# Depthwise-separable 1x1 convolution: the weight-scaling prologue re-ordered, one transfer on another queue

## The chip, the cores and the metric

The kernel runs on one core of a Trainium2 chip. Its engines are TensorE (matrix multiplication, PE in the profile, with its weight loads as PEld), VectorE (DVE), ScalarE (ACT), GpSimd (POOL) and SyncE (SP, which here issues most transfers). The metric is the device time of one execution in microseconds; less is better. Before the change it is 573.41 us, the median of three runs (573.28 to 573.43).

## The reference

The input `x` is a bf16 image of 384 x 384 pixels with 384 channels, `dw` holds one factor per channel (a depthwise kernel of size 1), and `pw` is a 384 x 384 matrix:

```
out = x * dw[0, 0][None, None, None, :]      # depthwise, k = 1
out = einsum('bhwc,cd->bhwd', out, pw)       # pointwise
```

So the result is, for 147456 pixels, a row of 384 channels times a 384 x 384 matrix whose rows are scaled by `dw`.

## The kernel before, in words

The scaling is folded into the weights: the kernel first forms `w_r`, the rows of `pw` times `dw`, in an order that suits the main loop, and then multiplies `x` by it.

The main loop goes over 288 supertiles of 512 pixels. A supertile is loaded as a part of a chunk of `x` (chunks of 1, 1, 1, 1, 2, 4, 5, 5 and then 10 supertiles, at the end smaller ones again) into one of three buffers `X`. VectorE transposes it in 32 x 32 blocks of 32-bit words into one of two tiles `T` (`transposes`, L348 to L380); one instruction makes half a supertile, three of the six pairs of channel blocks. Only the first supertile's first half is made in three single blocks (L370 to L372), so that TensorE can begin after the first of them. TensorE then runs `supertile` (L220): 12 steps of 4 matmuls, each with 32 rows of the array and 384 columns, into four banks of one of the two PSUM tiles `PS`. ScalarE copies the four banks out as bf16 (L434), and SyncE issues the store. The order on each engine is the order in which the code issues to it; the semaphores hold the engines together. There is no planner.

Ahead of the loop stands a prologue of a few microseconds:

- ScalarE's queue loads `dw` (L183), SyncE's queue loads the first 128 rows of `pw` (L184), then the other 256 (L185, semaphore `s_pw2`), then the chunks of `x` (`load_x`, L133), one after the other.
- GpSimd makes an identity `eye`; VectorE sums it into the selector `sel` (L395, which raises `s_dwf` to 1).
- TensorE runs dummy matmuls over a constant (`idle_work`, L244; each pass is four matmuls): four passes, then, when `dw` has landed, three tiny matmuls that turn the row `dw` into columns of PSUM (L260), then three more passes.
- VectorE copies those columns from PSUM to `dw_f` (L402, `s_dwf` to 2) and makes three scaled selectors `sel_w`, one for each 128 rows of `pw` (L405, `s_sw`).
- TensorE multiplies `sel_w` and `pw` (L280), six products (k, r) for k in 0 to 2 and r in 0 and 1. The products (1, 1) and (2, 0) are run twice. Each leaves two banks of PSUM, and raises `s_w`.
- ScalarE and VectorE copy the products from PSUM into `w_r` (`w_out`, L387, with the copy on L390). The list of units and engines is `w_units` (L175): unit 0 on ScalarE, 1 on VectorE, 2 on ScalarE, the fourth product in two halves, one on ScalarE and one, `(3, 1, 2, 0)`, on VectorE, then 4 and 5 on ScalarE.
- VectorE then goes on with the first two supertiles' transposes. The loop's first matmul waits for the units of the first four products on both engines (`w_first`, `w_after(3)`) and for the first transposed block (`s_t[0][0]`).

The PSUM bank that held the columns of `dw` is also written by product (0, 0). Because each engine works in order, an instruction that waits on VectorE or on SyncE's queue holds all that is issued behind it there.

Of the kernel before, what the change touches and what calls it, by code (L numbers as in the profile page):

```python
# [26 lines left out]
def kernel(  # L27
# [12 lines left out]
    nc = tc.nc  # L40
    P = nc.NUM_PARTITIONS
    B, H, W, C = x.shape
    assert dw.shape[0] == 1 and dw.shape[1] == 1, "only k=1 depthwise supported"
    D = pw.shape[1]
# [29 lines left out]
    pw_n = raw[:, 0 : 3 * D].rearrange("p (k d) -> p k d", d=D)  # L74
    sel_w = raw[:, 3 * D :].rearrange("p (k r q w) -> p k r q w", r=2, q=4, w=32)
    w_k = raw[:, 0 : 2 * D].rearrange("p (r d) -> p r d", d=D)
    eye = consts.tile([P, P], BF16, name="eye")
    sel = consts.tile([P, 2, 32], F32, name="sel")
    w_r = consts.tile([P, NB, 2, D], BF16, name="w_r")
    dw_row = consts.tile([1, C], BF16, name="dw_row")  # L80
    dw_f = consts.tile([P, 3], F32, name="dw_f")
# [9 lines left out]
    PS = [psum.tile([P, 4, 512], F32, name=f"ps{s}") for s in range(2)]  # L91
# [13 lines left out]
    s_pw2 = nc.alloc_semaphore("s_pw2")  # L105
    s_df = nc.alloc_semaphore("s_df")
    s_sw = nc.alloc_semaphore("s_sw")
    s_dwf = nc.alloc_semaphore("s_dwf")
# [4 lines left out]
    with tc.tile_critical(sync_engine=mybir.EngineType.Pool, no_gpsimd_drain=True) as section:  # L113
        def x_of(t):
            g, i, off, first, L = chunks[t]
            if first + 2 == NS:
                return Xl[:], s_xl, 32
            n = sum(len(ls) > i for ls in groups[g % NR : g + 1 : NR])
            return Xs[g % NR][:, 4 * off : 4 * (off + L), :], s_x[g % NR][i], 16 * n

        def load_x(t, eng=nc.sync):
            g, i, off, first, L = chunks[t]
            dst, sem, _ = x_of(t)
            rows = xf[512 * first : 512 * (first + L), :]
            if first + 3 < NS:
                src = rows.rearrange("(p s) c -> p (s c)", p=P)
                dst = dst.rearrange("p s c -> p (s c)")
                if i == 0 and g >= NR:
                    je = g_end[g - NR]
                    eng.wait_ge(s_t[je % 2][1], je // 2 + 1)  # L130
            else:
                src = rows.rearrange("(a k q) c -> q a k c", k=4, q=4)
            eng.dma_start(dst, src).then_inc(sem, 16)  # L133
# [43 lines left out]
        def w_after(i):  # L177
            n = [sum(u[3] == e and u[0] <= i for u in w_units) for e in range(2)]
            return [(s_wr[e], n[e]) for e in range(2)]
# [2 lines left out]

        nc.scalar.dma_start(dw_row[:], dw.rearrange("a e c -> a (e c)")).then_inc(s_dw, 16)  # L183
        nc.sync.dma_start(pw_n[:, 0], pw[0:P, :]).then_inc(s_pw, 16)  # L184
        nc.sync.dma_start(pw_n[:, 1:3], pw[P:C, :].rearrange("(k p) d -> p k d", p=P)).then_inc(s_pw2, 16)  # L185
        load_x(0)

        todo = []
# [25 lines left out]
        def w_ps(i):  # L214
            return PS[0 if i in (2, 3) else 1][:, 2 * (i % 2) : 2 * (i % 2) + 2, :D]
# [28 lines left out]
        def idle_work(n):  # L244
            for _ in range(n):
                for i in range(4):
                    nc.tensor.matmul(  # L247
                        PS[0][:, 2 * (i % 2) + i // 2, :D],
                        lhsT=ones[32 * i : 32 * i + 32, 0:P],
                        rhs=ones[32 * i : 32 * i + 32, :],  # L250
                        start=True,
                        stop=True,
                        tile_position=(32 * i, 0),
                    )
# [3 lines left out]
        nc.tensor.wait_ge(s_dw, 16)  # L258
        for k in range(3):
            mm = nc.tensor.matmul(  # L260
                PS[1][:, 0, D + k : D + k + 1],
                lhsT=dw_row[:, P * k : P * k + P],
                rhs=ones[0:1, 0:1],
                start=True,
                stop=True,
            )
        mm.then_inc(s_df)
        idle_work(3)
        nc.tensor.wait_ge(s_pw, 16)
        times = {(1, 1): 2, (2, 0): 2}  # L270
        for k in range(3):
            if k == 1:
                nc.tensor.wait_ge(s_pw2, 16)
            nc.tensor.wait_ge(s_sw, k + 1)
            for r in range(2):
                if k == 2:
                    nc.tensor.wait_ge(*w_after(r)[1 - r])

                for v in [0, 1] * times.get((k, r), 1):
                    mm = nc.tensor.matmul(  # L280
                        PS[(k + 1) % 2][:, 2 * r + v, :D],
                        lhsT=sel_w[64 * v : 64 * v + 64, k, r, :, :].rearrange("p q w -> p (q w)"),
                        rhs=pw_n[64 * v : 64 * v + 64, k, :],
                        start=True,
                        stop=True,
                        tile_position=(64 * v, 0),
                    )
                mm.then_inc(s_w)
# [59 lines left out]
        def transposes(t, j):  # L348
            g, i, off, first, L = chunks[t]
            jj = first + j  # L350
            s = jj % 2
            if jj + 1 == NS:
                nc.vector.wait_ge(s_xk, 32)
                Tw = Ts[s][:].bitcast(U32).rearrange("p b (m w) -> p (b m) w", w=32)
                for v in range(2):
                    blocks = slice(12 * v, 12 * v + 12)
                    ins = nc.vector.transpose(out=Tw[:, blocks], in_=Xk[:, blocks].bitcast(U32))  # L357
                    ins._wait_ge(s_pe, 2 * (jj - 2) + v + 1)
                    ins.then_inc(s_t[s][v])
                return  # L360
            X, sem, n = x_of(t)
            Xw = X.bitcast(U32).rearrange("p (k l) c -> p k l c", l=L)
            Tw = Ts[s][:].bitcast(U32).rearrange(
                "p b (k i) -> p b k i" if t < 2 else "p b (i k) -> p b k i", k=4
            )
            for h in range(2):
                if h == 0 and j == 0:
                    nc.vector.wait_ge(sem, n)
                if h == 0 and jj == 0:
                    for b in range(3):  # L370
                        x_b = Xw[:, :, 0, 32 * b : 32 * b + 32]
                        nc.vector.transpose(out=Tw[:, b], in_=x_b).then_inc(s_tb if b else s_t[0][0])  # L372
                    continue
                ins = nc.vector.transpose(  # L374
                    out=Tw[:, 3 * h : 3 * h + 3],
                    in_=Xw[:, :, j, 96 * h : 96 * h + 96].rearrange("p k (b w) -> p b k w", w=32),
                )
                if jj >= 2:
                    ins._wait_ge(s_pe, 2 * (jj - 2) + h + 1)
                ins.then_inc(s_t[s][h])  # L380
# [6 lines left out]
        def w_out(i, v0, v1, e):  # L387
            k, r = i // 2, i % 2
            out, in_ = w_r[:, 2 * k + v0 : 2 * k + v1, r, :], w_ps(i)[:, v0:v1]
            o = nc.vector.tensor_copy(out, in_) if e == 0 else nc.scalar.copy(out, in_)  # L390
            o._wait_ge(s_w, i + 1)
            o.then_inc(s_wr[e])
# [5 lines left out]
            op=mybir.AluOpType.add,  # L398
            axis=mybir.AxisListType.X,
        ).then_inc(s_dwf)  # L400
        nc.vector.wait_ge(s_df, 1)
        nc.vector.tensor_copy(dw_f[:], PS[1][:, 0, D : D + 3]).then_inc(s_dwf)  # L402
        nc.vector.wait_ge(s_dwf, 2)
        for k in range(3):
            nc.vector.tensor_scalar_mul(  # L405
                sel_w[:, k], sel[:].unsqueeze(2).to_broadcast([P, 2, 4, 32]), dw_f[:, k : k + 1]
            ).then_inc(s_sw)
        for u in w_units:
            w_out(*u)
        transposes(*order[0])  # L410
        transposes(*order[1])

        for jj, (t, j) in enumerate(order):
# [29 lines left out]
            if jj + 2 < NS:  # L443
                transposes(*order[jj + 2])
# [35 lines left out]
```

## Time and profile before

| what | value |
|---|---|
| median of three runs | 573.41 us |
| the profiled execution | 573.63 us |
| its span, first to last instruction | 571.7 us |
| TensorE busy (matmuls) | 566.9 us |
| VectorE busy | 507.9 us |
| ScalarE busy | 418.4 us |
| bytes moved by the transfers | 226.88 MB, mean 397 GB/s |
| first matmul of the main loop | 6.45 us after the span's start |

The times are of one profiled execution, counted from its first instruction. In the rows of the order of time the first number is the start and the second the duration, then come engine, line, operation, output and inputs with their shapes, the number of instructions merged into the row, and in brackets the engine's idle time before it with what ended that. A `q` behind an engine's name marks an instruction of its queue that issues a transfer; it is not counted as busy time, and its duration is that of the issue, not of the transfer. Ends of matmuls are modelled, so a matmul's duration is longer than the distance to the next one. In the rows of groups, busy time and mean duration stand behind the bar.

### The profile page before, as it was taken

The page shows a single profiled execution, that of the slowest core. Times are in us where ns is not written, and L with a number is a line of the kernel's source. Part 1 is how long each engine was busy: PE and PEld are TensorE (multiplying, and loading weights), DVE is VectorE, ACT ScalarE, POOL GpSimd, SP SyncE. Part 2 cuts the span into 40 slices and gives each one's busy share as a digit, 9 for nine tenths or more (in the row PEclk, how much of TensorE's full clock was granted, in tenths as well). Part 3 has the DMA queues.
Part 4 walks back from the last instruction along what each step waited for, and adds up shares of the span by engine and source line. Part 5 has one row for each costly group of instructions (what it writes and reads, how often), then busy time and mean ns, then how long its engine had stood idle before and what let it go on. Part 6 is the DMA issues. An engine that isn't in the chain of part 4 may idle for free.

```text
span 571.7 us, 29724 instructions
## 1 busy us (share of the span) xinstructions
PE 566.9 (99%) x13847; PEld 414.4 (72%) x13847; DVE 507.9 (89%) x589; ACT 418.4 (73%) x298; POOL 13.9 (2%) x41
## 2 busy tenths in 40 slices
PE   8999999999999999999999999999999999999997
PEld 5777777777777777777777777777777777777775
DVE  7889889889889889899899898898898898898896
ACT  6777777777777777777777777777777777777775
POOL 2042000000000000000000000000000000000000
PEclk9999999999999999999999999999999999999999
DMA  8999999999999999999999999999999999998777
GB/s 320 440 385 390 434 422 429 433 421 418 421 439 414 399 405 425 403 393 393 434 387 390 408 413 404 407 411 412 406 404 415 402 395 397 423 393 330 307 286 270
DMA packets 28084, 226.88 MB, mean 397 GB/s; under 512 B 1449, under 2 KB 7850, under 8 KB 24106
## 3 DMA queue, kind: packets, MB, share of 16 engines
q1 hardware_dynamic: 27140, 225.91, 97.6%
q10 hardware_dynamic: 934, 0.89, 0.4%
q14 instruction: 9, 0.07, 0.0%
q8 instruction: 1, 0.02, 0.0%
HBM read 113.54 MB, written 113.25 MB: 397 GB/s over the span
## 4 chain that ended last, share of the span: by engine, by line
PE 99%; DVE 0%; ACT 0%; issue 0%
PE ps L230 98%; PE ps L247 0%; DVE w_r L390 0%; PE ps L315 0%; PE ps L280 0%; PE ps L303 0%; ACT O L429 0%; DVE T L372 0%; PE ps L260 0%
## 5 line engine op out<-in xcount | busy, mean ns | idle before, releaser
L230 PE MATMUL ps<-w_r,T 32*128 32x384 bf16 x13776 | 559.8, 321 | 0.3 <-DVE T L372 0.3
L374 DVE STREAM_TRANSPOSE T<-X 128x384 uint32<-128x384 uint32 x571 | 499.5, 876 | 55.2 <-DMA X<-in_x_dram 0.5
L230 PEld LDWEIGHTS ps<-w_r,T 32*128 32x128 bf16 x13776 | 411.3, 93 | 148.8 <-issue 0.9
L434 ACT CAST O<-ps 128x1536 bf16<-128x1536 f32 x286 | 411.7, 1440 | 146.6 <-PE ps L230 146.6
L344 POOL COPY Xk<-Xl 32x256 bf16<-32x256 bf16 x16 | 6.3, 396 | 0.0
L343 POOL COPY Xk<-Xl 32x128 bf16<-32x128 bf16 x16 | 4.6, 289 | 24.8 <-DMA Xl<-in_x_dram 24.0
L390 ACT CAST w_r<-ps 128x768 bf16<-128x768 f32 (+1 forms) x5 | 3.3, 754 | 1.2 <-PE ps L280 1.2
L247 PE MATMUL ps<-const-bfloat16-1.0 32*128 32x384 bf16 x28 | 2.7, 514 | 1.1 <-PEq L464 1.1
L338 POOL COPY raw<-w_r 32x768 bf16<-32x768 bf16 x4 | 3.3, 821 | 6.5 <-ACT w_r L390 6.3
L346 ACT ACT_TABLE_LOAD x1 | 1.3, 1283 | 1.5 <-PEq L464 1.5
L280 PE MATMUL ps<-raw 64*128 64x384 bf16 x16 | 2.4, 466 | 0.0
L425 DVE CAST O<-ps 128x384 bf16<-128x384 f32 x2 | 1.0, 554 | 1.4 <-PE ps L230 1.4
L280 PEld LDWEIGHTS ps<-raw 64*128 64x128 bf16 x16 | 1.0, 126 | 1.6 <-issue 1.3
L390 DVE CAST w_r<-ps 128x768 bf16<-128x768 f32 (+1 forms) x2 | 1.5, 758 | 0.7 <-PE ps L280 0.7
L247 PEld LDWEIGHTS ps<-const-bfloat16-1.0 32*128 32x128 bf16 x28 | 0.9, 121 | 1.6 <-issue 1.4
L374 DVE STREAM_TRANSPOSE T<-Xl 128x384 uint32<-128x384 uint32 x2 | 1.8, 882 | 0.2
L395 DVE TENSOR_REDUCE sel<-eye 128x64 f32<-128x128 bf16 x1 | 0.3, 289 | 1.5 <-POOL eye L325 1.5
L357 DVE STREAM_TRANSPOSE T<-Xk 128x384 uint32<-128x384 uint32 x2 | 1.2, 578 | 0.5 <-PE ps L230 0.4
L429 ACT CAST O<-ps 128x384 bf16<-128x384 f32 x2 | 1.0, 480 | 0.7 <-PE ps L315 0.7
L315 PE MATMUL ps<-raw,T 128*128 128x384 bf16 x8 | 1.5, 328 | 0.0
L429 DVE CAST O<-ps 128x384 bf16<-128x384 f32 x2 | 1.1, 558 | 0.1
L424 ACT CAST O<-ps 128x384 bf16<-128x384 f32 x2 | 0.9, 482 | 0.5 <-PE ps L230 0.5
(14 smaller groups left out, 5.1 us busy)
## 6 DMA issues: line engine op xcount, KB each, us to landing
X<-in_x_dram SPq DMA_DIRECT2D x25, 3840.0 KB, 21.8
out_dram<-O SPq DMA_DIRECT2D x25, 3840.0 KB, 27.7
X<-in_x_dram SPq DMA_DIRECT2D x3, 1536.0 KB, 18.5
X<-in_x_dram SPq DMA_DIRECT2D x2, 1920.0 KB, 14.5
out_dram<-O SPq DMA_DIRECT2D x2, 1920.0 KB, 24.0
out_dram<-O SPq DMA_DIRECT2D x2, 1536.0 KB, 13.0
X<-in_x_dram SPq DMA_DIRECT2D x6, 384.0 KB, 5.8
out_dram<-O SPq DMA_DIRECT2D x3, 768.0 KB, 5.7
```

Of the source, the lines that this page charges most:

```text
L230: mm = nc.tensor.matmul(PS[s][:, q, :D], lhsT=Ts[s][32 * q : 32 * q + 32, b, par::2], rhs=w_r[32 * q : 32 * q + 32, b, par, :], start=(b, ...
L247: nc.tensor.matmul(PS[0][:, 2 * (i % 2) + i // 2, :D], lhsT=ones[32 * i : 32 * i + 32, 0:P], rhs=ones[32 * i : 32 * i + 32, :], start=True ...
L280: mm = nc.tensor.matmul(PS[(k + 1) % 2][:, 2 * r + v, :D], lhsT=sel_w[64 * v : 64 * v + 64, k, r, :, :].rearrange("p q w -> p (q w)"), rhs ...
L315: mm = nc.tensor.matmul(PS[1][:, m, :D], lhsT=Tk[:, P * (m + 2) : P * (m + 3), par], rhs=w_k[:, par, :], start=False, stop=par == 1,)
L338: nc.gpsimd.tensor_copy(w_k[quads[n]], w_r[quads[n], n]).then_inc(s_wk)
L343: nc.gpsimd.tensor_copy(Xk[quads[n], g:8:4, :], x_b).then_inc(s_xk)
L344: nc.gpsimd.tensor_copy(Xk[quads[n], 8 + g : 24 : 4, :], Xl[quads[g], :, 64 * n : 64 * n + 64]).then_inc(s_xk)
L346: nc.scalar.copy(warm[:, s : s + 1], nc.const_aps.tensor(0.0, [P, 1], F32)).then_inc(s_a[s])
L374: ins = nc.vector.transpose(out=Tw[:, 3 * h : 3 * h + 3], in_=Xw[:, :, j, 96 * h : 96 * h + 96].rearrange("p k (b w) -> p b k w", w=32),)
L390: o = nc.vector.tensor_copy(out, in_) if e == 0 else nc.scalar.copy(out, in_)
L429: o = (nc.scalar.copy if n % 2 else nc.vector.tensor_copy)(Ov[:, n, j, :], PS[s][:, n, :D])
L434: a = nc.scalar.copy(Ov[:, :, j, :], PS[s][:, :, :D])
```

## The change

Six edits, all in the prologue:

1. The last 256 rows of `pw` are loaded from ScalarE's queue, behind `dw`, instead of SyncE's.
2. SyncE waits until VectorE's sum is done (`s_dwf` at 1) before it issues the first chunk of `x`; all later issues on that queue come behind it.
3. The columns of `dw` go to bank 2 of the second PSUM tile instead of bank 0, which product (0, 1) overwrites.
4. The second group of dummy passes has two instead of three.
5. VectorE scales the first selector with the column of `dw` taken from PSUM, then copies the columns to `dw_f`, then scales the other two from `dw_f`. Product (0, 1) waits until the copy is done (`s_dwf` at 2).
6. VectorE's half unit `(3, 1, 2, 0)` is issued behind the first transposed block instead of ahead of it.

```diff
-        nc.sync.dma_start(pw_n[:, 1:3], pw[P:C, :].rearrange("(k p) d -> p k d", p=P)).then_inc(s_pw2, 16)
+        nc.scalar.dma_start(pw_n[:, 1:3], pw[P:C, :].rearrange("(k p) d -> p k d", p=P)).then_inc(s_pw2, 16)
+        nc.sync.wait_ge(s_dwf, 1)
         load_x(0)
...
-                PS[1][:, 0, D + k : D + k + 1],
+                PS[1][:, 2, D + k : D + k + 1],
...
-        idle_work(3)
+        idle_work(2)
...
             for r in range(2):
+                if (k, r) == (0, 1):
+                    nc.tensor.wait_ge(s_dwf, 2)
...
                         nc.vector.transpose(out=Tw[:, b], in_=x_b).then_inc(s_tb if b else s_t[0][0])
+                        if b == 0:
+                            w_out(3, 1, 2, 0)
...
+        def scale(k, by):
+            sel_b = sel[:].unsqueeze(2).to_broadcast([P, 2, 4, 32])
+            nc.vector.tensor_scalar_mul(sel_w[:, k], sel_b, by[:, k : k + 1]).then_inc(s_sw)
+
+        dw_p = PS[1][:, 2, D : D + 3]
+        nc.vector.wait_ge(s_dwf, 1)
         nc.vector.wait_ge(s_df, 1)
-        nc.vector.tensor_copy(dw_f[:], PS[1][:, 0, D : D + 3]).then_inc(s_dwf)
+        scale(0, dw_p)
+        nc.vector.tensor_copy(dw_f[:], dw_p).then_inc(s_dwf)
         nc.vector.wait_ge(s_dwf, 2)
-        for k in range(3):
-            nc.vector.tensor_scalar_mul(
-                sel_w[:, k], sel[:].unsqueeze(2).to_broadcast([P, 2, 4, 32]), dw_f[:, k : k + 1]
-            ).then_inc(s_sw)
+        scale(1, dw_f)
+        scale(2, dw_f)
         for u in w_units:
-            w_out(*u)
+            if u[:2] != (3, 1):
+                w_out(*u)
```

## The prediction

> **What bounds the kernel now.** I read the busy shares first, then the chain of waits, then the order of time over the first 14 us. The page's first lines:
>
> ```profile
> span 571.7 us, 29724 instructions
> ...
> PE 566.9 (99%) x13847; PEld 414.4 (72%) x13847; DVE 507.9 (89%) x589; ACT 418.4 (73%) x298; POOL 13.9 (2%) x41
> ```
>
> TensorE is busy in 99% of the span. The chain that ended last, in order of time (start, duration, what), says where the rest lies:
>
> ```profile
> 4.62 0.96 DVE w_r L390
> ...
> 5.58 0.56 DVE w_r L390
> 6.13 0.23 DVE T L372
> 6.36 0.09 issue
> 6.45 559.85 PE ps L230 x13776
> 566.30 0.65 PE ps L303 x16
> ```
>
> From 6.45 to 566.30 us the chain is one uninterrupted piece: 13776 matmuls in 559.85 us, 40.6 ns each, so 48 of them (one supertile) take 1.95 us. Nothing in the diff touches that loop or what follows it. The end therefore moves exactly as the loop's first matmul moves, unless the change opens a hole later. The whole question is the 6.45 us in front, where the last links are VectorE's: two evacuations of the scaled weights (L390), then the first transposed block (L372), then 0.10 us of hand-over.
>
> The profiled execution took 573.63 us, 0.22 above the median 573.41. I make the sum against the trace and apply the difference to the median. What a measurement here can tell from no change is about 0.2%, 1.15 us; everything this diff can shorten lies well below that.
>
> **The path to 6.45, in order of time.**
>
> ```profile
> 0.97 0.54 ACTq L183 DMA_DIRECT2D dw_row<-in_dw_dram  x1
> ...
> 1.41 0.41 SPq L185 DMA_DIRECT2D raw<-in_pw_dram  x1
> 1.48 0.29 DVE L395 TENSOR_REDUCE sel<-eye 128x64 f32<-128x128 bf16 x1 [1.48 <-POOL eye L325]
> 1.54 1.28 ACT L346 ACT_TABLE_LOAD   x1 [1.54 <-PEq L464]
> ...
> 2.84 0.28 ACT L346 COPY warm<-const-float32-0.0 128x1 f32<-128x1 f32 x2
> 2.88 0.16 DVE L402 COPY dw_f<-ps 128x3 f32<-128x3 f32 x1 [1.11 <-PE ps L260]
> 3.07 0.88 DVE L405 TENSOR_SCALAR raw<-sel,dw_f 128x256 bf16<-128x256 f32 x3
> ...
> 4.05 0.15 PEld L280 LDWEIGHTS ps<-raw 64*128 64x128 bf16 x2 [0.17 <-DMA raw<-in_pw_dram]
> 4.30 3.29 ACT L390 CAST w_r<-ps 128x768 bf16<-128x768 f32 x5 [1.18 <-PE ps L280]
> 4.37 0.15 PEld L280 LDWEIGHTS ps<-raw 64*128 64x128 bf16 x2 [0.17 <-issue]
> 4.62 1.52 DVE L390 CAST w_r<-ps 128x768 bf16<-128x768 f32 x2 [0.66 <-PE ps L280]
> ...
> 6.66 0.54 DVE L374 STREAM_TRANSPOSE T<-X 128x384 uint32<-128x384 uint32 x1
> 7.70 6.70 DVE L374 STREAM_TRANSPOSE T<-X 128x384 uint32<-128x384 uint32 x9 [0.50 <-DMA X<-in_x_dram]
> ```
>
> **Dummy pass and first product** (one answer for both). Three short stretches of TensorE's order of time, and the group of the three scalings:
>
> ```profile
> 2.62 0.89 PE L247 MATMUL ps<-const-bfloat16-1.0 32*128 32x384 bf16 x8
> ...
> 2.91 0.91 PE L247 MATMUL ps<-const-bfloat16-1.0 32*128 32x384 bf16 x8
> 3.75 0.50 PE L280 MATMUL ps<-raw 64*128 64x384 bf16 x2
> ...
> L405 DVE TENSOR_SCALAR raw<-sel,dw_f 128x256 bf16<-128x256 f32 x3 | 0.9, 349 | 0.0
> ```
>
> The first row is passes one and two, ending at 3.51; the second is passes two and three, ending at 3.82. The first real product starts at 3.75, while its scaled selector was finished at 3.07 + 0.35 = 3.42 (0.88 for three of 0.35: one every 0.27). So the third dummy pass, not VectorE, holds it: one pass fewer is worth 3.82 - 3.51 = 0.31 us, and the product can start at 3.44 if its selector is there. With today's scaling it would come too late (3.42 and the 0.10 of hand-over make 3.52). With the scalar read from PSUM the scaling starts where the copy started, 2.88, and ends at 3.23, 0.19 earlier. What a scalar from PSUM costs no row shows: by the copy, which reads PSUM in 0.16, nothing extra; at worst that whole 0.16, which gives 3.39 + 0.10 = 3.49. I take nothing extra, since one column is read. So 3.44, with 0.05 as the far end. The copy follows at 3.15 and the second scaling at 3.34, where it stands today (3.07 + 0.27): no change. The added wait of product (0,1) is for that copy, over at 3.31, against its turn at about 3.73: hidden by 0.4.
>
> All products then move up by 0.31 as long as pw's last 256 rows are there: (0,0) 3.44, (0,1) 3.74, (1,0) 4.06, then the doubled (1,1) and (2,0) at a pitch of 0.32, the distance between the weight loads at 4.05 and 4.37.
>
> **pw's last rows on ScalarE's queue.** Sizes and landings now, issue to landing:
>
> ```profile
> X<-in_x_dram SPq DMA_DIRECT2D x6, 384.0 KB, 5.8
> ...
> raw<-in_pw_dram SPq DMA_DIRECT2D x1, 192.0 KB, 2.5
> raw<-in_pw_dram SPq DMA_DIRECT2D x1, 96.0 KB, 2.0
> ...
> DMA to landing us min/median/max: 3.7/3.7/3.7
> ...
> DMA to landing us min/median/max: 5.3/5.3/5.3
> ```
>
> The last two rows are x's first chunk (issued 1.88, landed 5.58) and the second (issued 2.38, landed 7.68). pw's 192 KB land at 1.41 + 2.5 = 3.91 today. On ScalarE the issue comes behind dw's, which ends at 1.51: 1.55, 0.14 later. ScalarE pays 0.41 of issue: its table load ends at 3.24 and the two small copies at 3.52, before its first evacuation at 3.99; cover 0.47, so nothing. Early bound of the landing: 1.55 + 2.35 = 3.9. Late bound: it shares the engines with x's first chunk all the way, and lands a little ahead of it, 5.0. The engines were indeed loaded in that time (stretch, length, granted clock, DMA share, GB/s):
>
> ```profile
> 2.00:3.00 1.00, 1.00 0.70 165
> 3.00:4.00 1.00, 1.00 1.01 277
> 4.00:5.00 1.00, 1.00 1.07 304
> 5.00:6.00 1.00, 1.00 0.94 347
> ```
>
> Until 3 there is room, after that none. I take 4.3, nearer the early end, because this transfer has a head start of 0.27 on x's. Then (1,0) starts at 4.4, about where it is now, instead of 4.06. ScalarE's evacuations follow: (0,0) at 3.44 + 0.55 = 3.99 (today 3.75 to 4.30), the third unit at 4.4 + 0.55 = 4.95, and the half unit behind it:
>
> ```profile
> 4.99 0.80 ACT L390 CAST w_r<-ps 128x768 bf16<-128x768 f32 x1
> ...
> 5.68 0.50 ACT L390 CAST w_r<-ps 128x384 bf16<-128x384 f32 x1
> ...
> 6.05 0.30 DVE L372 STREAM_TRANSPOSE T<-X 128x128 uint32<-128x128 uint32 x1
> 6.28 0.46 DVE L372 STREAM_TRANSPOSE T<-X 128x128 uint32<-128x128 uint32 x2
> ```
>
> A pitch of 0.69 and then 0.50 give 4.95 + 0.69 + 0.50 = 6.14; with 0.10 the loop starts no earlier than 6.24. In general that is landing + 1.94: break-even with 6.45 at a landing of 4.51.
>
> **x's first chunk waits for VectorE's sum.** The sum ends at 1.48 + 0.29 = 1.77, so the issue goes out at about 1.82, 0.06 before today's 1.88, and every later chunk and store behind it on SP's queue moves by no more than that. Without the wait it would have gone at 1.41. No pw rows are now in front of it on its own queue. Bounds of its landing: as pw's 192 KB (2.5) plus 192 KB more at 347 GB/s (0.55), so 4.9; or, when both transfers split the engines and the mix is worse than today's order, 5.58 + 0.3 = 5.9. I take 5.35: the total of bytes is the same, and the share of 0.70 before 3 us leaves about 0.3 us of engine time that the second queue can fill.
>
> **Half an evacuation behind the first transposed block.** VectorE's first evacuation moves to 4.30 and ends at 5.26 (0.96). Then comes the block (the next instruction starts 0.23 behind it, 6.05 to 6.28) and only then the half unit (0.56). The loop waits for both, so it starts at block start + 0.23 + 0.56 + 0.10 = + 0.89. With a landing at 5.35 the block starts at 5.37 and the loop at 6.26. Were the chunk no obstacle: 5.26, loop at 6.15. If it lands at 5.58 as now, 5.60, loop at 6.49, 0.04 worse than today: what was cover for a late chunk (the half evacuation stood in front) has become a queue behind it. The other blocks keep their cover: the supertile's second half (0.54 long, 0.61 behind the first block today, 0.47 more with the half evacuation between) is complete 1.62 after the first block's start, and TensorE needs it half a supertile after its own start, 0.89 + 0.98 = 1.87.
>
> **Sum.** The later of 6.24 and 6.26 against 6.45: -0.19 us. The next thing to be late is x's second chunk: VectorE idled 0.50 for it, transposed it until 8.28, and TensorE wants it at 6.45 + 1.95 = 8.40, leaving some 0.03 after hand-over. It landed 2.1 after the first although 384 KB at 347 GB/s are 1.1, so about 1 us of that was a delay I don't expect each time; without it there is no hole.
>
> **The clock.** The products at 4.05 and 4.37 stand 0.32 us apart, the loop's matmuls four in 0.16. By form of the product (min/median/max ns), early ones and the last four:
>
> ```profile
> L280 PE MATMUL ps<-raw x10: 496/524/524, 3.8 to 5.0; 64*128 64x384 bf16 x10
> ...
> L280 PE MATMUL ps<-raw x4: 322/325/330, 5.6 to 5.8; 64*128 64x384 bf16 x4
> ```
>
> TensorE thus doubled its pace near 5.6 us, although the granted clock reads 1.00 throughout. The dummy passes kept it busy up to there. The change takes 0.31 of that work away, and a late pw adds a wait of up to 0.3.
> The Trainium skill (TensorE: Matmul & The Clock Gate, "What's actually happening") says that the array starts at half rate and is released after a busy window of about 3.4 us, whose phase is not tied to the kernel; the trace agrees with the doubling, and by that rule a thinner window could postpone it by a whole 3.4 us, the rival "cold" below.
>
> **Rivals.**
> - *Late weights* (slower than before). The 192 KB on the second queue are served in turn with x's bigger packets and land after 4.51. At 4.8 the loop starts at 6.74: +0.29, 573.70; at 5.0, +0.49, 573.90. For it: DMA share above 1.0 from 3 to 5. Against: the head start. The Trainium skill (DMA: Bandwidth & Descriptors, "Issuing engines are not separate DMA queues") says that another issuing engine saves only issue time and the transfers interleave on the same engines; the shares fit that, and by it alone the move would bring no earlier data at all.
> - *Cold.* TensorE's holes in front of 5.6 are enough to leave it at half pace. If the doubling came 3.4 later, at 9.0, the loop would run from about 6.4 to 9.0 at half pace and lose 1.3: 573.41 + 1.3 - 0.1 = 574.6. For it: fewer dummies and one new hole. Against: with holes of about 0.2 and 0.3 the stretch from 2.6 to 5.6 remains nearly full.
> - *Second chunk binds.* It lands at 7.68 again; TensorE waits in front of its second supertile, and at most 0.03 is left: 573.4, the same as no effect.
> - *All of it.* Both x chunks and pw land early: 6.15, -0.30, or a little more: 573.1.
>
> **How the numbers follow.** My forecast, a gain near 0.19 us, gets 0.38; all of it 0.13; second chunk 0.17; late weights 0.25; cold 0.07. The likeliest gives 573.41 - 0.19 = 573.22. The range reaches from 572.95 (the full gain plus the runs' own spread of 0.15) to 573.90 (weights at 5.0); it leaves out the cold case and thin tails. By the 0.2% bound all but the cold case are no change: same 0.91; slower 0.07, from the cold case; faster 0.02, for something not thought of, since the most that can be removed in front of the loop is about 0.3.
>
> **What would show it.** First product at 3.44 and its scaling at 2.88; pw's second landing below 4.5; the first block before 5.5 with the half evacuation behind it; the loop's first matmul near 6.26; no idle time of TensorE at 8.2. Wrong if the weight load behind pw's landing waits past 4.4, if VectorE idles for x's first chunk past 5.6, or if the loop's first matmuls stand 0.32 apart instead of 0.16.

## The result and the profile after

The changed kernel takes 576.88 us in the median (576.21 to 577.04 over six runs) against 573.42 for the kernel before on the same chip: a ratio of 1.0049, 95% interval 1.0035 to 1.0062. It is slower: by 3.5 us in the medians, by 2.0 to 3.6 us by that interval. The profiled execution took 576.21, the lowest of the six, 2.6 above the profiled execution of before; those 2.6 us are accounted for below.

The first lines of the page and the chain of waits of the changed kernel (start, duration, what):

```profile
span 574.2 us, 29717 instructions
...
PE 568.0 (99%) x13843; PEld 345.7 (60%) x13843; DVE 509.5 (89%) x589; ACT 418.4 (73%) x298; POOL 13.9 (2%) x41
...
1.54 4.35 DMA raw<-in_pw_dram
5.89 0.05 issue
5.94 2.10 PE ps L283 x12
8.04 560.85 PE ps L231 x13300
568.89 0.65 PE ps L306 x14
```

The chain now runs through a transfer that was not on it before: pw's last 256 rows, issued at 1.54 and landed 4.35 us later. And the loop is longer: from its first matmul, at 7.97, to its end, at 568.89, it takes 560.92 instead of 559.85. (The chain counts the loop from 8.04, where the modelled end of the last product lies.) Lines of the order of time, same kernel (the loop is L231, products L283, evacuations L395, transposed blocks L375, scalings L408, the copy L414):

```profile
1.54 0.41 ACTq L185 DMA_DIRECT2D raw<-in_pw_dram  x1
...
1.79 6.40 SPq L133 DMA_DIRECT2D X<-in_x_dram  x9
...
2.75 0.36 DVE L408 TENSOR_SCALAR raw<-sel,ps 128x256 bf16<-128x256 f32 x1 [0.99 <-PE ps L261]
3.03 0.15 DVE L414 COPY dw_f<-ps 128x3 f32<-128x3 f32 x1
...
3.26 0.82 PE L283 MATMUL ps<-raw 64*128 64x384 bf16 x4
...
5.75 0.31 DVE L375 STREAM_TRANSPOSE T<-X 128x128 uint32<-128x128 uint32 x1 [0.68 <-DMA X<-in_x_dram]
...
5.94 2.10 PE L283 MATMUL ps<-raw 64*128 64x384 bf16 x12 [1.86 <-DMA raw<-in_pw_dram]
...
7.12 0.56 DVE L395 CAST w_r<-ps 128x384 bf16<-128x384 f32 x1 [1.05 <-PE ps L283]
...
7.97 3.22 PE L231 MATMUL ps<-w_r,T 32*128 32x384 bf16 x48
...
8.27 0.16 PEld L231 LDWEIGHTS ps<-w_r,T 32*128 32x128 bf16 x4 [0.16 <-DVE T L375]
8.59 0.16 PEld L231 LDWEIGHTS ps<-w_r,T 32*128 32x128 bf16 x4 [0.16 <-issue]
...
9.87 0.16 PEld L231 LDWEIGHTS ps<-w_r,T 32*128 32x128 bf16 x4 [0.16 <-issue]
10.19 0.78 PEld L231 LDWEIGHTS ps<-w_r,T 32*128 32x128 bf16 x20 [0.16 <-issue]
```

Up to 3.8 us the steps of VectorE and TensorE are earlier than before: the first product starts at 3.26 instead of 3.75. Then TensorE stands idle for 1.86 us until pw's rows land, does the other twelve matmuls at half pace, and the loop begins at 7.97 instead of 6.45: +1.52. The groups of four weight loads at 8.27, 8.59 and on to 9.87 stand 0.32 apart; from 10.19 twenty of them fit in 0.78. So the loop's first 2.2 us also run at half pace, which costs +1.07 over its 13776 matmuls. 1.52 + 1.07 = 2.59: the loop ends at 568.89 instead of 566.30. Of the same kernel's executions above 576.21 one more was profiled (e11 below).

The end of the rows' transfer stands among the transfers between 4.3 and 5.3 us (queue, packets, MB, share of the 16 engines):

```profile
q1 hardware_dynamic: 140, 0.39, 98.5%
q10 hardware_dynamic: 28, 0.02, 5.5%
```

q1 is SyncE's queue, with x's packets of 3072 bytes; q10 is ScalarE's, with pw's packets of 768 bytes. x has nearly the whole of the engines, and the rest of pw's packets trickle out beside it: 230 of the 256 had begun before 4.3. The transfer signals its landing in sixteen parts: twelve had landed by 4.74, the last two at 5.75 and 5.89. That x's company is the cause is shown by e3 below.

### The profile page after: what moved, and what is told of

The parts are those of the page before. It is cut to its first block, busy times and chain, and to the rows that moved or that the text cites. A ratio compares the mean times of both kernels' runs of the same rounds, so it can differ in the third digit from the quotient of the medians.

```text
span 574.2 us, 29717 instructions
## 1 busy us (share of the span) xinstructions
PE 568.0 (99%) x13843; PEld 345.7 (60%) x13843; DVE 509.5 (89%) x589; ACT 418.4 (73%) x298; POOL 13.9 (2%) x41
## 4 chain that ended last, share of the span: by engine, by line
PE 98%; DMA 1%; ACTq 0%; ACT 0%; issue 0%; POOLq 0%
PE ps L231 98%; DMA raw<-in_pw_dram 1%; PE ps L283 0%; PE ps L318 0%; PE ps L306 0%; ACTq L183 0%; ACT O L440 0%; ACTq L486 0%; POOLq L113 0%; POOLq L475 0%
## 5 line engine op out<-in xcount | busy, mean ns | idle before, releaser
L231 PE MATMUL ps<-w_r,T 32*128 32x384 bf16 x13776 | 560.9, 321 | 0.0
L231 PEld LDWEIGHTS ps<-w_r,T 32*128 32x128 bf16 x13776 | 343.0, 93 | 218.2 <-issue 1.6
L395 ACT CAST w_r<-ps 128x768 bf16<-128x768 f32 (+1 forms) x5 | 3.5, 738 | 2.2 <-PE ps L283 2.1
L283 PE MATMUL ps<-raw 64*128 64x384 bf16 x16 | 2.9, 516 | 1.9 <-DMA raw<-in_pw_dram 1.9
L283 PEld LDWEIGHTS ps<-raw 64*128 64x128 bf16 x16 | 0.9, 126 | 3.8 <-DMA raw<-in_pw_dram 3.2
L395 DVE CAST w_r<-ps 128x768 bf16<-128x768 f32 (+1 forms) x2 | 1.5, 758 | 1.3 <-PE ps L283 1.3
L375 DVE STREAM_TRANSPOSE T<-X 128x128 uint32<-128x128 uint32 x3 | 0.8, 294 | 0.7 <-DMA X<-in_x_dram 0.7
```

Source lines behind the costliest of these rows:

```text
L231: mm = nc.tensor.matmul(PS[s][:, q, :D], lhsT=Ts[s][32 * q : 32 * q + 32, b, par::2], rhs=w_r[32 * q : 32 * q + 32, b, par, :], start=(b, ...
L283: mm = nc.tensor.matmul(PS[(k + 1) % 2][:, 2 * r + v, :D], lhsT=sel_w[64 * v : 64 * v + 64, k, r, :, :].rearrange("p q w -> p (q w)"), rhs ...
```

## The experiments

The theory after the result: pw's rows, on a queue of their own, share the transfer engines with x's bulk packets and land late (contention); the hole that this makes in TensorE's work holds back the release of its clock (cold). Rivals: ScalarE's queue is slow by itself; the thinner dummy work alone leaves the clock at half pace; the half evacuation behind the block costs the time; an extra price of the scalar in PSUM.

Where the profiled executions stood (us; "rows" is the landing of pw's last rows, "chunk" that of x's first chunk; the loop is taken from its first matmul to its end; a ratio is to the kernel before, with its 95% interval, and is not the ratio of the two medians; e11 to e15 are single executions):

| kernel | rows | chunk | loop starts | loop takes | profiled | median | ratio |
|---|---|---|---|---|---|---|---|
| before | 3.90 | 5.57 | 6.45 | 559.85 | 573.63 | 573.41 | |
| after | 5.89 | 5.73 | 7.97 | 560.92 | 576.21 | 576.88 | 1.0049 [1.0035, 1.0062] |
| e1 rows back on SyncE | 3.87 | 6.33 | 7.35 | 559.83 | 574.50 | 573.88 | 1.0006 [0.9995, 1.0017] |
| e2 queue alone | 5.53 | 4.49 | 7.64 | 561.17 | 576.21 | 575.83 | 1.0041 [1.0027, 1.0055] |
| e3 x behind pw | 4.10 | 5.97 | 7.00 | 559.83 | 574.14 | 574.14 | 1.0011 [1.0001, 1.0020] |
| e4 hole filled | 6.23 | 6.41 | 8.29 | 559.83 | 575.43 | 576.54 | 1.0053 [1.0037, 1.0070] |
| e5 first product alone | 3.89 | 5.27 | 6.00 | 560.48 | 573.79 | 573.79 | 1.0007 [0.9998, 1.0017] |
| e6 order alone | 4.21 | 5.29 | 6.32 | 559.83 | 573.63 | 573.88 | 1.0005 [0.9996, 1.0014] |
| e7 one pass fewer | 5.14 | 6.09 | 7.24 | 561.26 | 575.83 | 573.37 | 0.9995 [0.9986, 1.0004] |
| e8 pw in one | 4.10 | 5.07 | 6.85 | 560.54 | 574.71 | 574.51 | 1.0015 [1.0006, 1.0024] |
| e9 hole alone | 4.51 | 5.48 | 8.03 | 560.99 | 576.48 | 576.23 | 1.0044 [1.0027, 1.0061] |
| e10 hole alone, filled | 3.92 | 6.08 | 7.67 | 559.83 | 576.49 | 576.37 | 1.0042 [1.0028, 1.0056] |
| e11 after, again | 6.52 | 6.59 | 8.60 | 560.19 | 576.37 | | |
| e12 hole filled, again | 6.27 | 6.14 | 8.02 | 559.83 | 576.76 | | |
| e13 the same | 6.13 | 5.94 | 8.45 | 559.83 | 577.28 | | |
| e14 the same | 6.31 | 6.22 | 8.45 | 559.83 | 577.13 | | |
| e15 hole alone, filled, again | 4.44 | 5.64 | 7.67 | 559.83 | 575.76 | | |
| e16 filled, shorter program | 6.53 | 6.37 | 8.28 | 559.83 | 575.42 | 575.51 | 1.0033 [1.0020, 1.0046] |
| e17 full-row passes | 3.91 | 5.78 | 6.36 | 559.83 | 573.52 | 573.59 | 1.0000 [0.9990, 1.0010] |
| e18 e5, full-row passes | 3.78 | 5.47 | 6.14 | 560.73 | 574.19 | 573.70 | 1.0000 [0.9990, 1.0010] |

**e1: the whole change without the move of pw's rows.**

```diff
-        nc.scalar.dma_start(pw_n[:, 1:3], ...)
+        nc.sync.dma_start(pw_n[:, 1:3], ...)
```

> The changed kernel with one part undone: pw's last 256 rows go back to SyncE's queue, ahead of x's first chunk. Theory 'contention on the second queue' (x's packets, served in turn on the same engines, delay those rows): they land near 3.9 us again, the loop's first matmul comes between 6.1 and 6.5, and the time is 573.1 to 573.5. Rival 'too little dummy work' (the clock doubles late because one pass is missing): the loop still starts at half pace, 574.4 or more. Rival 'half evacuation behind the block': the loop starts above 6.6, 573.6 or more.

**e2: that move alone, in the kernel before.**

```diff
-        nc.sync.dma_start(pw_n[:, 1:3], ...)
+        nc.scalar.dma_start(pw_n[:, 1:3], ...)
```

> The kernel before with one part done alone: pw's last 256 rows on ScalarE's queue; x's first chunk is then issued at once, near 1.41 us. Theory 'contention on the second queue': the rows land at 5.9 us or later, since x's packets are now in front of them from the start; TensorE idles about 2 us in front of product (1,0), the loop starts at half pace, and the time is 575.9 to 577.5. Rival 'too little dummy work': all seven passes are there, so at most the wait remains, 574.9 to 575.2. Rival 'half evacuation behind the block': no loss, 573.4.

The chain of e1 with a line of VectorE's order of time, and then the chain of e2:

```profile
5.73 1.51 ACT w_r L395 x2
...
7.35 559.83 PE ps L231 x13776
```

```profile
6.58 0.52 DVE L395 CAST w_r<-ps 128x384 bf16<-128x384 f32 x1
```

```profile
1.53 4.00 DMA raw<-in_pw_dram
5.53 0.05 issue
5.58 2.10 PE ps L280 x12
7.68 561.13 PE ps L230 x13772
```

With the rows back on SyncE's queue they land 2.5 us after their issue, the loop runs at full pace, and the median is not to be told from the kernel before. The expected start of the loop, 6.1 to 6.5, was missed: x's first chunk landed at 6.33, the half evacuation behind the first block ended at 7.10, and the loop began at 7.35, as the rival 'half evacuation behind the block' had it. (The chain names ScalarE's copies that ended at 7.24, but by the code the loop's first matmul does not wait for those two.) By the interval all edits but the move cost 0.17% at most.

The move alone gives 575.83, most of the whole loss, with the same three links in the chain: rows 4.00 us after their issue, twelve matmuls at half pace, a loop that is 1.3 too long. The rows landed at 5.53, not at 5.9 or later as expected, and the median lies just below the expected 575.9. e2 still has all seven dummy passes, the old order on VectorE and the old scaling. So the thinner dummy work, the order and the scalar in PSUM are not needed for this loss. The profiled executions of e2 and of the whole change took the same 576.21; why the medians differ, 575.83 and 576.88, stays open.

**e3: x's first chunk held back until pw's first rows have landed**, all else as changed.

```diff
-        nc.sync.wait_ge(s_dwf, 1)
+        nc.sync.wait_ge(s_pw, 16)
         load_x(0)
```

> The changed kernel, but SyncE waits for the landing of pw's first 128 rows (3.0 us) instead of VectorE's sum before it issues x's first chunk, so the rows on ScalarE's queue have the engines to themselves for about 1.2 us. Theory 'contention on the second queue': they land at 3.8 to 4.0; x's first chunk lands at 6.2 to 6.7, the loop starts at 7.1 to 7.6 at full pace, 574.1 to 574.7. Rival 'ScalarE's queue is slow in itself': they land at 5.5 or later, and the time is above 576.

The chain of e3:

```profile
1.53 2.57 DMA raw<-in_pw_dram
...
4.15 1.80 PE ps L283 x7
...
7.00 559.83 PE ps L231 x13776
```

The same issue from the same ScalarE queue now lands in 2.57 us instead of 4.35, because x was issued at 2.94 instead of 1.79. ScalarE's queue is not slow; the company of x's bulk is what delays it. The loop is late now by x's chunk (5.97), and the median 574.14 lies 0.1% above the kernel before.

How the company acts is only partly seen. From 2.9 to 3.3 us, in the changed kernel and then in e3:

```profile
q10 hardware_dynamic: 66, 0.05, 77.8%
q1 hardware_dynamic: 3, 0.01, 8.0%
```

```profile
q10 hardware_dynamic: 124, 0.09, 77.6%
```

The same share of the engines moved half as many of pw's packets while x's chunk had been issued, although only 3 packets of q1 ran beside them. And in e2, where x was issued first, x's chunk landed whole at 4.49 and the first of the rows' sixteen parts at 4.53. So a plain alternation of pw's packets with x's is not what the traces show; the order in which the engines serve the two queues stays open.

**e9: the hole without a late transfer.** In the kernel before, product (1, 0) also waits for eight copies that GpSimd makes one after another, until 5.87 us. **e10** puts six dummy passes into that hole.

```diff
+        for i in range(8):
+            if i:
+                nc.gpsimd.wait_ge(s_hole, i)
+            nc.gpsimd.tensor_copy(pad[:], ones[:, 0:D]).then_inc(s_hole)
...
             if k == 1:
+                idle_work(6)                  # e10 only
                 nc.tensor.wait_ge(s_pw2, 16)
+                nc.tensor.wait_ge(s_hole, 8)
```

> The kernel before; all transfers as before. Product (1,0) also waits until GpSimd has made eight small copies into a tile that nothing else uses (about 6.1 us), so TensorE has a hole of 1.5 to 2 us that no transfer causes. Theory 'late rows and half pace are two separate losses': the loop starts 2.05 us after the wait's end, 1.3 to 2.0 later than before, and it runs its first 0.5 to 3.5 us at half pace, 0.3 to 1.8 more: 575.3 to 577.3. Rival 'the half pace belongs to the transfers': only the later start, 574.8 to 575.6.

> The same wait on GpSimd, with six dummy passes (1.92 us) in the hole. Theory: the loop starts at most 0.4 later than with the open hole and runs at full pace from its first matmul, or at half pace for less than 0.5 us; 575.0 to 575.9, and 0.5 to 1.3 less than with the open hole. Rival 'the half pace belongs to the transfers': no difference between the two.

The chain of e9:

```profile
5.97 2.10 PE ps L283 x12
8.07 560.95 PE ps L232 x13776
```

A hole of 1.60 us with no transfer behind it gives the same two losses: the loop starts at 8.03, and takes 1.1 too long. So the half pace follows from the hole, whatever made it. In e10 the pace doubled at 4.0 us and the loop took 559.83; yet the median, 576.37, missed the expected 575.0 to 575.9 and is no lower than that of e9. In the profiled execution the last store landed 1.5 us later than usual. That needed an explanation of its own.

**e4, e12, e13 and e14: the hole of the changed kernel filled** with seven dummy passes, one kernel executed four times. **e15** is e10 again, **e11** the changed kernel again.

```diff
             if k == 1:
+                idle_work(7)
                 nc.tensor.wait_ge(s_pw2, 16)
```

> The changed kernel with seven dummy passes (2.24 us at the early pace) between products (0,1) and (1,0), where TensorE idled 1.86 us; the rows still land near 5.9. Theory 'the hole kept the clock down': TensorE doubles its pace before the loop starts, the loop starts near 8.0 (at most 0.2 later than in the changed kernel) at full pace, and the time falls by about 1.0 to 1.5 against the changed kernel, to 575.0 to 575.9. Rival 'the loss is the late rows alone': no less than 576.2.

> The changed kernel once more, for the spread of two moments between executions: the landing of pw's last rows (5.9 us in the first profile) and the end of the half pace (10.2). Theory 'x's packets on slow transfer engines': the landing lies anywhere from 5.2 to 7.5; theory 'the clock is released by a full window whose phase is not tied to the kernel': the pace doubles anywhere from 8.6 to 12.

> The changed kernel with seven dummy passes in the hole once more (e4). Its profiled execution took 575.43, three others 576.3 to 576.8. Theory 'the rows land later in those': here they land after 6.5, TensorE waits for them behind the passes, and the loop starts after 8.5. Rival 'dummy work does not keep the clock up': the rows land before 6.4 and the loop still starts at half pace.

> The changed kernel with seven dummy passes more between the products of (0,1) and of (1,0), looked at a third time. If the hole costs through the pace alone, the 13300 matmuls of the main loop take 559.8 instead of 560.8 and the profiled time is the start of the loop (7.9 to 8.6) plus 559.8 plus 7.3, so 575.0 to 575.8. If something at the end takes it back, the loop still takes 559.8 but the tail behind it is over 8.5 instead of 7.3 and the time is 576.3 to 577.0; the last stores would then land over 3 us after their issue, or their issue would be late. If the pace is what varies, the loop takes over 560.3.

> The same kernel a fourth time, the same three cases: 575.0 to 575.8 with a tail of 7.3 behind the loop; 576.3 to 577.0 with a tail over 8.5; or a loop over 560.3.

> The kernel before with the hole made by GpSimd and six dummy passes in it, looked at again. With the tail of the kernel before (7.3 behind the loop) it would take 574.7 to 575.6, with the loop starting at 7.6 to 8.4 and taking 559.8; with the late end seen in its first execution 576.3 to 577.0.

e11 took 576.37 with the rows landing later still, at 6.52, the loop starting at 8.60 and only 0.3 too long: the lateness and the half pace vary from execution to execution, one against the other. In e12 the rows landed at 6.27, so a later landing is not what kept the time up. All four profiled executions of the filled kernel had a loop of 559.83, as the cold theory says. But they took 575.43, 576.76, 577.28 and 577.13: only the first gave the microsecond back, and e4's median of 576.54 is what the rival 'the late rows alone' expected. e15 took 575.76, between its two expected cases, with a loop of 559.83 as well. The transfers from 570 to 574 us, of e13 and then of e4:

```profile
q1 hardware_dynamic: 541, 0.63, 46.7%
q10 hardware_dynamic: 144, 0.10, 7.9%
q8 instruction: 1, 0.02, 1.7%
...
out_dram<-O ACTq DMA_DIRECT2D x1, 96.0 KB, 3.5
```

```profile
q1 hardware_dynamic: 503, 0.58, 41.4%
q10 hardware_dynamic: 144, 0.10, 7.8%
...
out_dram<-O ACTq DMA_DIRECT2D x1, 96.0 KB, 1.9
```

In e13 a packet of instructions, 16 KB on queue q8, lies among the last stores, from 572.01 to 573.12; the last store lands 3.5 us after its issue instead of 1.9, its final packets one after another behind that one. In e4 the same packet came at 574.12, after the last store. It lay at 568.0 to 572.0, among the stores, in e10, e12, e14 and e15 too, and in none of the fourteen other profiled executions: those without a filled hole, and e16 to e18. The passes that fill the hole make TensorE's program longer, and the kernel seems to reach the point where this block is fetched a little sooner.

**e16 takes that apart.** It is e4 with every dummy pass written as one matmul over 128 rows instead of four over 32 rows, so that TensorE's program is shorter than that of the changed kernel. **e17** is the control, the kernel before with its passes written so. **e18** is e5 (below) with its passes written so. Dummy passes write only PSUM that is overwritten later, so nothing of the output depends on them.

```diff
-                for i in range(4):
-                    nc.tensor.matmul(PS[0][:, 2 * (i % 2) + i // 2, :D],
-                        lhsT=ones[32 * i : 32 * i + 32, 0:P], rhs=ones[32 * i : 32 * i + 32, :], ...)
+                nc.tensor.matmul(PS[0][:, 0, :D], lhsT=ones[:, 0:P], rhs=ones[:, :], ...)
```

> The changed kernel with the hole filled by seven dummy passes, as before, but every dummy pass is one matmul over 128 rows instead of four over 32 rows each, so that TensorE's program is shorter than that of the changed kernel and not longer. If the late end of the filled kernels comes from their longer program (a 16 KB transfer of instructions that falls among the last stores), there is none here and the tail behind the loop is 7.3: with the loop at full pace (559.8) and its start at 7.9 to 8.6 the median is 575.0 to 575.8, 1.1 to 1.9 below the changed kernel's 576.88. If the late end belongs to the filling itself, 576.3 to 577.3 again. If passes in this form don't release the clock, the loop takes over 560.3 and the time is over 575.8 with a tail of 7.3.

> The kernel before with its seven dummy passes as one matmul over 128 rows each, nothing else: 573.2 to 573.8 if the form of a dummy pass makes no difference; over 574.2, with a loop over 560.3, if passes in this form don't release the clock in time.

> The kernel before with the first scaling from PSUM, a copy behind it and one dummy pass fewer, and dummy passes of one matmul over 128 rows each. With passes over 32 rows its loop began at 6.00 and ran 0.6 too long. If denser dummy work releases the clock before the loop: start 5.9 to 6.1, loop 559.8, 573.0 to 573.3, the one tried version below the kernel before. If the release comes at its own time, the loop takes 560.2 to 560.6 again and the time is 573.5 to 574.0.

The chain of e16 and its transfers from 570 to 574:

```profile
1.54 4.99 DMA raw<-in_pw_dram
...
8.28 559.83 PE ps L231 x13776
```

```profile
q1 hardware_dynamic: 498, 0.57, 41.0%
q10 hardware_dynamic: 144, 0.10, 7.9%
...
out_dram<-O ACTq DMA_DIRECT2D x1, 96.0 KB, 1.9
```

Although the rows landed as late as 6.53, the median is 575.51 and all six runs lie between 575.31 and 575.76, as expected if the late end came from the longer program. The sum closes: start +1.83, loop -0.02, 573.63 + 1.81 = 575.44 against 575.42 measured. e17 is the kernel before to 0.1%. So the loss has two parts, of which e16 takes one away: 1.85 us remain with the late start alone (e16 against the 573.66 of before beside it), and the other 1.4 go with the half pace (576.88 against 575.51; two separate comparisons, and e16's rows landed later than those of the changed kernel's profile, so the split is rough).

**e5: the first product's edits alone** (columns of dw in the other bank, scaling from PSUM, one pass fewer), **e7: one pass fewer alone**, **e6: the order on VectorE alone**, each in the kernel before. **e8** is e5 with all of pw in one transfer.

```diff
# e7
-        idle_work(3)
+        idle_work(2)
# e6
                         nc.vector.transpose(out=Tw[:, b], in_=x_b).then_inc(s_tb if b else s_t[0][0])
+                        if b == 0:
+                            w_out(3, 1, 2, 0)
# e8, on top of e5
-        nc.sync.dma_start(pw_n[:, 0], pw[0:P, :]).then_inc(s_pw, 16)
-        nc.sync.dma_start(pw_n[:, 1:3], ...).then_inc(s_pw2, 16)
+        nc.sync.dma_start(pw_n[:, 0:3], ...).then_inc(s_pw, 16)
```

> The kernel before with three parts of the change alone: the columns of dw in bank 2, the first selector scaled from PSUM, one dummy pass fewer. Theory 'the rest of the change is sound, only the queue and the swap cost': the first product starts near 3.27 to 3.45, the evacuations move up by 0.3, and the loop starts at 6.15 to 6.3 unless x's first chunk lands after 5.75, in which case its landing plus 0.4; the time is 0 to 0.3 below the kernel before. Rival 'too little dummy work': half pace in the loop, 1.0 or more above the kernel before.

> The kernel before with VectorE's half evacuation behind the first transposed block, nothing else. Theory: the loop then starts at the block's start plus 1.04 (0.23 to the half unit, 0.56 for it, 0.25 of hand-over, as in the trace of the changed kernel, since TensorE's two further waits come after this one), or x's landing plus 1.06: 6.6 to 7.3, 0.2 to 0.6 above the kernel before. Rival 'VectorE has slack': no difference.

> The kernel before with one dummy pass fewer, nothing else. Theory: the first product is then held by its selector (about 0.2 after dw's copy and scaling), so it comes 0 to 0.25 earlier; the time is within 0.25 of the kernel before. Rival 'too little dummy work': 1.0 or more above it.

> The kernel of the three sound parts (e5), with pw loaded by one transfer on SyncE's queue instead of two, so that x's first chunk is issued near 1.41 instead of 1.88. The first product then waits for all of pw, landing 3.3 to 3.7, at most 0.3 later than in e5; x's first chunk lands 0.2 to 0.5 earlier than there. If x's landing binds e5, this is faster than e5 by 0.1 to 0.3; if pw binds, slower by up to 0.2.

The chain of e5, of e7, and two lines of TensorE's order of time with one of VectorE's of e18:

```profile
3.30 2.74 PE ps L282 x16
6.04 560.44 PE ps L230 x13776
```

```profile
1.41 3.73 DMA raw<-in_pw_dram
...
5.18 2.10 PE ps L280 x12
7.29 561.22 PE ps L230 x13184
```

```profile
6.14 2.13 PE L230 MATMUL ps<-w_r,T 32*128 32x384 bf16 x48 [0.31 <-DVE T L372]
8.99 3.27 PE L230 MATMUL ps<-w_r,T 32*128 32x384 bf16 x76 [0.72 <-DVE T L374]
```

```profile
8.26 3.99 DVE L374 STREAM_TRANSPOSE T<-X 128x384 uint32<-128x384 uint32 x6 [1.38 <-DMA X<-in_x_dram]
```

The profiled execution of e5 starts its loop 0.45 us earlier and gives 0.63 back in it, since the pace doubled only at 7.4: without late rows the start can be gained, and here the clock took it. Its median, 573.79, was expected 0 to 0.3 below that of before and is not. e18, with denser passes, had its pace double at 5.3 and kept the full pace, but in the profiled execution x's second chunk landed at 8.24 and TensorE idled 0.72 for it; its median, 573.70, is that of before, and not the expected 573.0 to 573.3. e6 and e7 change nothing that can be measured. The one profiled execution of e7 is its slowest (575.83, median 573.37): there the rows landed at 5.14 although they were on SyncE's queue, since two of their sixteen parts were late, and the same chain followed, with the same half pace. e8 is 0.15% slower: one transfer for all of pw holds the first product back to 4.15, and in the profiled execution the loop ran 0.69 too long. No version tried is faster than the kernel before beyond its uncertainty.

## Why the prediction was wrong

**What bounds the kernel**: right in its form. The first matmul of the loop moved by 1.52, and the end by 2.59: the loop's own length, taken as fixed "unless the change opens a hole later", grew by 1.07, from a hole that opened in front of it.

**First product**: right, and a little better than forecast: 3.26 against 3.44. The scaling from PSUM took 0.36 where one from `dw_f` took 0.35, so "nothing extra" holds; it began at 2.75 because dw's columns were there sooner. That part is luck: with the old scaling and all passes the first product came at 3.55 in e2, e6, e9 and e10, against 3.75 in the profile of before, so about 0.3 of the 0.49 belongs to the edits, as forecast. The wait of product (0, 1) was hidden, and ScalarE's issue of 0.41 was covered, as said.

**pw's last rows on ScalarE's queue**: this is the step that failed. I took a landing of 4.3 with 5.0 as the late bound; it was 5.89, and 5.53 to 6.53 in the other executions that share this queue with an early x. The late bound assumed that both transfers share the engines and that pw "lands a little ahead of" x's chunk. Where pw was issued 0.25 us ahead of x, the two landed together: the rows 0.16 behind the chunk in the first profile (5.89 against 5.73), and from 0.2 ahead of it to 0.2 behind it in e4, e11 to e14 and e16; in e2, with x issued first, the rows came 1.04 behind. And the chunk itself, for which the prediction allowed up to 5.9, landed at 5.73 to 6.59 in those. A fair late bound from the rows shown would have been the bound of x's own landing, 5.9, and not 5.0. The head start of 0.27, on which 4.3 rested, bought nothing that the traces show. The rule of "landing + 1.94" stands: 5.89 + 1.94 = 7.83 against 7.97, and 5.53 + 1.94 = 7.47 against 7.64 in e2. Its price for the true landing is +1.4, nearly three times the +0.49 of my bound.
The Trainium skill (DMA: Bandwidth & Descriptors, "Issuing engines are not separate DMA queues") was cited for "no earlier data at all". The runs agree as far as the shares of both queues add up to about the whole of the engines (98.5% and 5.5% from 4.3 to 5.3 us), and go further: the data came 2.0 us later than from the shared queue (5.89 against 3.90).

**The clock**: the mechanism was named, its condition and price were not. I priced "cold" at 7% as a case beside late weights, with holes of 0.2 and 0.3. But late weights make the hole, one of 1.86 us: in every execution with rows that late and the hole not filled the half pace came with them, so the two rivals should have been one, at 25% and more, and worth 2.5 to 3. The doubling came at 10.2 in the changed kernel against 5.6 before. The price of 1.3 for a doubling at 9.0 was for a loop that begins at 6.4; the loop's own extra, 1.07, was measured.
The Trainium skill (TensorE: Matmul & The Clock Gate, "What's actually happening") has the release behind a busy window of about 3.4 us that runs freely. The moments of doubling fit it: 4.0 to 7.4 us in the profiled executions where TensorE had no long hole among its products, and 8.3 to 10.4 in those six where it idled 0.85 to 2.49 us there, unfilled (e8 0.85 and 8.3, e7 0.99 and 10.2, e2 1.21 and 10.4, e9 1.60 and 10.4, after 1.86 and 10.2, e11 2.49 and 9.4). A longer hole did not mean a later doubling, and where the hole lies matters: in e1 TensorE idled 1.34 us and in e3 0.75 behind all its products, directly in front of the loop, and both loops ran at full pace from the first matmul.

**x's first chunk**: the issue came at 1.79 (forecast 1.82), and the landing at 5.73, inside the bounds of 4.9 to 5.9 though not at 5.35; in the six other profiled executions with both queues as changed it was 5.94 to 6.59, outside them. It was no longer what held the loop.

**Half an evacuation behind the block**: the order does as described, but its hand-over was mis-sized: 0.10 taken from a loop that waited for a transposed block. Where the half evacuation ends last, the loop begins 0.25 behind its end in e1, e3 and e6, and 0.29 in the changed kernel, where the half evacuation waited for its product and not for the block. So "+ 0.89" is 1.0: 5.31 to 6.32 in e6, 6.35 to 7.35 in e1.

**Second chunk binds**: not seen in the changed kernel, whose loop began too late for it; seen in e18, whose loop began at 6.14 and waited 0.72 for a second chunk that landed at 8.24.

**The remainder.** The median lies 0.67 above the profiled execution. A landing of 6.52 as in e11 with a doubling at 10.2 would give most of it: start +2.15, half pace (10.2 - 8.6) / 2 = 0.8, in all 576.6. That is worked out and was not observed in one execution; the cause of the remainder stays open.

## What to carry to other kernels

A small load that the start of a kernel waits for should not be put on a queue beside a bulk load that is issued at about the same time: ahead of the bulk on one queue it took mostly 2.5 us here (2.4 to 3.7), beside it 4.0 to 5.0. When a late operand opens a hole among the first matmuls ahead of a long TensorE loop, price it together with what the hole does to the clock, not as a case of its own. And a saving of a few tenths of a microsecond at the start can be worth nothing, as in the profiled execution of e5, when the pace doubles only later.

## What was not expected of the hardware

- The same 192 KB took mostly 2.5 us from issue to landing on the queue ahead of x (3.7 in e7), 2.57 on ScalarE's queue with x held back, and 4.0 to 5.0 on it with x under way.
- The moment at which the matmuls double their pace differs between executions by several microseconds: 4.0 in e10 and 7.4 in e5, and of one and the same kernel 4.5 in e12 and 7.4 in e13, none with a hole of more than half a microsecond in front. The granted clock in the tables by stretch reads 1.00 throughout, so only the distances between instructions show it.
- Two late parts out of sixteen can make a short transfer late: in e7 fourteen parts of the rows had landed by 3.87, and the landing came at 5.14.
- A 16 KB packet of instructions among the last stores delays the store whose packets stand behind it by about 1.6 us (e13); 24 or 28 dummy matmuls more, near the start of the program, were enough to bring it there in five of the six profiled executions of such kernels, all but e4's. That the longer program is what brings it is supported by e16, whose shorter one had no such packet near the end, and not shown beyond that.
